# All block products by seven smaller ones, on seeded PSUM quarters, with adds on GpSimd and by DMA

## The chip, the cores and the metric

The kernel runs on one core of one Trainium2 chip. TensorE multiplies (its weight loads have a row of their own, PEld), VectorE (DVE) and ScalarE (ACT) do element-wise work and read and write PSUM, GpSimd (POOL) works on SBUF alone, and SyncE (SP) issues most DMAs; GpSimd and ScalarE issue the others. The metric is the device time in microseconds (us).

## The reference, cut to what matters

Hash attention makes x, of 4 batches x 768 tokens x 512 channels, and an MLP mixer follows, all in fp32:

```python
xt = x.transpose(0, 2, 1)
h = np.maximum(xt @ w_tok1, 0.0) @ w_tok2
u = x + h.transpose(0, 2, 1)
h2 = np.maximum(u @ w_ch1, 0.0) @ w_ch2      # w_ch1 [512, 1536], w_ch2 [1536, 512]
return (u + h2).astype(np.float32)
```

The change is all in the last two products, which the code calls the first and the second channel product.

## The kernel before, in words

The program has three stages: attention, token mixing and channels. Channels keeps u transposed in SBUF as XT (channels on partitions) and goes over its 3072 tokens in three stages s = 0, 1, 2 of 1024 tokens, two halves of 512 (TT).

**Block products.** A product of two matrices is cut in 2 x 2 blocks and made from seven block products, p1 to p7, instead of eight. Left operands are weights or sums of weight blocks (WC1 and SW1 for the first product, WC2 and SW2 for the second), right operands are token blocks or their sums (XT and T[0] to T[3], made by `inputs`). The partial sums come together by adds and by accumulation in PSUM. This can be done again inside a block product: then its left operand is seven smaller pieces, its right one has quarters b00 to b11 and four sums of them, and matmuls have 256 columns instead of 512.

**Stage s = 0, first product.** `hidden(0, t)`, t = 0 to 5, makes one row block of the hidden layer from seven block products of 2 instructions of 512 columns each (L806 to L822), in two pairs of PSUM banks (`blocks(2)`), and writes R[0] to R[3] with rectifiers. Between its parts it runs `jobs` from `prepare` (L1030): two lists of jobs to a t, one in the middle (L818) and one after. A job of `parts` (L1046) makes four sums of a weight's quarters on VectorE in a place, the one buffer `seen` or a free range of another tile, and SyncE stores them and the raw quarters in DRAM. Second-product parts are six (and p1 as a whole copy), first-product parts are the four names in SMALLER.

**Stages 1 and 2, first product.** `hidden_pair(s, t, between)`, t = 0 to 2, makes two row blocks at once: p1, p5 and p7 whole, in 4 instructions of 512 columns each (`whole`, L945), and p2, p6, p3, p4 by seven smaller ones each (class Smaller, L885), whose left pieces `fetch_hidden_left` brings from DRAM on SyncE's queue, five deep.

**Second product.** `outputs(s)` runs seven block products in the order p1, p5, p7, p6, p3, p2, p4. p1 is whole (`whole_product`, L1137, 12 instructions of 512 columns); in s = 0 it uses WC2 where it lies. The others are `product` (L1151): seven parts of 3 instructions of 256 columns in two pairs of banks, copies by ScalarE, adds and right sums by VectorE, and `fetch_left` of the product after the next. Results go to DRAM by accumulating DMAs from GpSimd's queue (`store`).

**Looks.** `look` brings a part of q or k in by a DMA from GpSimd's queue, and ScalarE squares and sums it (L1296, L1297); 32 of them are spread over hidden pairs and products. At the end they decide whether a careful version must run.

**Order.** Each engine runs its instructions in the order in which the code issues them; the waits between engines are put in by the framework, from what each instruction reads and writes. `accumulate` (L776) issues all matmuls of the channel stage, L779 in the profile.

Of the kernel before, what the change touches and what calls it, by code (L numbers as in the profile page):

```python
# [48 lines left out]
def kernel(  # L49
# [13 lines left out]
    nc = tc.nc  # L63
# [687 lines left out]
    def channels(pool, psum, SW1, second, TA, judge):  # L751

        KC, HC, QC = NCB // 2, NHT // 2, NHT // 4
        TB = pool.tile([P, 2, KC, TT], F32, name="TB", tag="TB", bufs=1)
        T = [TA[:, 0], TB[:, 0], TA[:, 1], TB[:, 1]]

        R = [pool.tile([P, 2, HC, TT // 2], F32, name=f"R{i}", tag=f"R{i}", bufs=1) for i in range(4)]
        q1 = pool.tile([P, KC, TT], F32, name="q1", tag="q1", bufs=1)
        last = B * S // (2 * TT) - 1

# [3 lines left out]

        ring = [0, 1, 2, 3]

# [3 lines left out]
        def blocks(n):  # L770

            now = ring[:n]
            ring[:] = ring[n:] + now
            return [bank_pair(i) for i in now]

        def accumulate(ps, left, right, ks, start=True, stop=True):  # L776
            ks = list(ks)
            for k in ks:
                nc.tensor.matmul(  # L779
                    ps, left(k), right(k), start=start and k == ks[0], stop=stop and k == ks[-1],  # L780
                    skip_group_check=True,
                )

        def copy(ps, c):
            nc.scalar.copy(c, ps)  # L785
            return c
# [3 lines left out]

        unfinished = []

        def end_rows():

            if unfinished:
                unfinished.pop()()

        def hidden(s, t):
# [6 lines left out]
            ps = [b[:, i] for b in blocks(2) for i in range(2)]  # L805
# [5 lines left out]
            p1 = copy(ps[0], c[0])  # L811
            p5 = copy(ps[2], c[1])
            accumulate(ps[0], lambda k: SW1[:, 0, k, low], lambda k: T[1][:, k], ks, False)
            p7 = copy(ps[3], c[2])
            end_rows()
            nc.vector.tensor_tensor(r[0], split(ps[1]), split(p1), op=ALU.add)
            nc.vector.tensor_scalar(r[0], r[0], 0.0, None, op0=ALU.max)
            for job in jobs.pop(0) if jobs else []:  # L818
                job()
# [3 lines left out]
            u = copy(ps[0], c[3])  # L823
            for k, a in [(3, p7), (1, ps[2]), (2, ps[3])]:
                nc.vector.tensor_tensor(r[k], split(a), split(u), op=ALU.add)
            nc.vector.tensor_scalar(r[1], r[1], 0.0, None, op0=ALU.max)

            def end():
                for k in (3, 2):
                    nc.scalar.activation(r[k], r[k], ACT.Relu)  # L830

            unfinished.append(end)
            nc.vector.tensor_tensor(r[1], r[1], r[0], op=ALU.subtract)

        def right_sums(name, s):


            sl = [slice(TT * (2 * s + i), TT * (2 * s + i) + TT) for i in range(2)]
            src = {"p2": XT[:, KC:, sl[0]], "p3": XT[:, KC:, sl[1]], "p6": T[1], "p4": T[3]}[name]
            z = split4(XT[:, SMALLER.index(name), : 2 * TT])  # L840
            half = [slice(0, TT // 2), slice(TT // 2, TT)]
            b = [src[:, k, n] for k in range(2) for n in half]

            def job():
                nc.vector.tensor_tensor(z[:, 0], b[1], b[0], op=ALU.subtract)
                nc.vector.tensor_tensor(z[:, 1], b[3], b[1], op=ALU.subtract)
                nc.vector.tensor_tensor(z[:, 2], b[3], z[:, 0], op=ALU.subtract)
                nc.vector.tensor_tensor(z[:, 3], b[2], z[:, 2], op=ALU.subtract)

            return job, [*b, *(z[:, i] for i in range(4))]  # L850

        def split4(a):
            return a.rearrange("p (n t) -> p n t", n=4)

        def fetch_hidden_left(h):

            if h < 4 * GP * last:
                t = h // 4 % GP
                nc.sync.dma_start(
                    out=hidden_left_at(h).rearrange("p (i c) -> p i c", i=7),  # L860
                    in_=hidden_passed[SMALLER[h % 4]][:, :7, P * t : P * t + P],
                )

        def hidden_left_at(h):

            h, n = h % 5, 7 * P
            if h < 3:
                return WC1[:, KC:].rearrange("p k c -> p (k c)")[:, n * h : n * h + n]
            return SW1[:, 2 * (h - 3)].rearrange("p k c -> p (k c)")[:, :n]
# [5 lines left out]
        def first_weight(name):  # L875

            return {
                "p2": WC1[:, KC:, : DCH // 2], "p3": SW1[:, 2], "p4": WC1[:, KC:, DCH // 2 :], "p6": SW1[:, 0],
            }[name]
# [5 lines left out]
        class Smaller:  # L885


            def __init__(self, h, name, s):
                self.h, self.w = h, hidden_left_at(h).rearrange("p (i c) -> p i c", i=7)
                self.b = right_sums(name, s)[1]  # L890

            def one(self, pair, e):

                self.ps, self.e = pair, split4(e)
                self.mm(pair[:, 0, : TT // 2], 4, 0)
                nc.scalar.copy(self.e[:, 0], pair[:, 0, : TT // 2])

            def three(self, pair, start=False):

                self.mm(pair[:, 0, : TT // 2], 5, 2, start)  # L900
                self.mm(pair[:, 0, TT // 2 :], 3, 3, start)
                self.mm(pair[:, 1, : TT // 2], 6, 7, start)

            def rest(self):

                self.mm(self.ps[:, 1, : TT // 2], 0, 4)
                self.mm(self.ps[:, 1, TT // 2 :], 1, 5)
                self.mm(self.ps[:, 0, : TT // 2], 2, 6, False)
                fetch_hidden_left(self.h + 5)

            def mm(self, ps, left, right, start=True):
                accumulate(ps, lambda k: self.w[:, left], lambda k: self.b[right], [0], start)

            def finish(self):

                u = extra_flat()[:, TT // 2 * (self.h % 2) : TT // 2 * (self.h % 2) + TT // 2]
                nc.scalar.copy(u, self.ps[:, 0, : TT // 2])
                p57 = self.ps[:, 1].rearrange("p (n t) -> p n t", n=2)
                nc.vector.tensor_tensor(
                    self.e[:, 1:3], p57, u[:, None, :].to_broadcast([P, 2, TT // 2]), op=ALU.add,  # L920
                )
                nc.vector.tensor_tensor(self.e[:, 3], p57[:, 0], self.e[:, 2], op=ALU.add)

        def hidden_pair(s, t, between):


            sl = [slice(TT * (2 * s + i), TT * (2 * s + i) + TT) for i in range(2)]
            ks = range(KC)
            r = [a[:, :, t::GP].rearrange("p n i c -> p i n c") for a in R]
            x, z, e, y = ring  # L930
            ring[:] = [y, e, x, z]

            p1, e2 = [output_at(i).rearrange("p i n -> p (i n)") for i in (0, 2)]
            p5, e6, u = copies(), copies(), copies()
            e3, e4 = p1, e2
            h = 4 * GP * (s - 1) + 4 * t
            p2, p6, p3, p4 = [Smaller(h + i, name, s) for i, name in enumerate(SMALLER)]

            def rows(a):
                return a.rearrange("p (i n c) -> p i n c", i=2, n=2)  # L940

            def banks(a):
                return a.rearrange("p i (n c) -> p i n c", n=2)

            def whole(pair, left, right, which=(0, 1)):  # L945
                for i in which:
                    at = P * (t + GP * i)
                    accumulate(pair[:, i], lambda k: left(k)[:, at : at + P], right, ks)

            def copy(to, pair):  # L950
                nc.scalar.copy(to.rearrange("p (i n) -> p i n", i=2), pair)

            def plus(to, a, b):
                nc.vector.tensor_tensor(to, a, b, op=ALU.add)

            def relu(i):
                nc.scalar.activation(r[i], r[i], ACT.Relu)

            X = bank_pair(x)
            whole(X, lambda k: WC1[:, k], lambda k: XT[:, k, sl[0]])  # L960
            Z, E = bank_pair(z), bank_pair(e)
            copy(p1, X)
            p2.one(E, e2)
            p2.three(Z, True)
            Y = bank_pair(y)
            whole(Y, lambda k: WC1[:, k, DCH // 2 :], lambda k: T[0][:, k], [0])
            n = TT * 3 // 2
            plus(p1[:, :n], Z.rearrange("p i n -> p (i n)")[:, :n], p1[:, :n])
            end_rows()
            p2.rest()  # L970
            whole(Y, lambda k: WC1[:, k, DCH // 2 :], lambda k: T[0][:, k], [1])
            p2.finish()
            copy(p5, Y)
            look()
            plus(r[0], rows(p1), rows(e2))
            for job in between:
                job()
            E = bank_pair(z)
            p6.one(E, e6)
            p6.three(X)  # L980
            copy(u, X)
            V = bank_pair(e)
            whole(V, lambda k: SW1[:, 1, k], lambda k: T[2][:, k])
            p6.rest()
            look()
# [488 lines left out]
```

## Time and profile before

| | |
|---|---|
| time, median of 3 runs | 797.19 us (797.18 to 799.81) |
| profiled execution: its time, its span | 795.77 us, 794.0 us |
| channel stage on TensorE (chain of waits) | 388.17 to 788.79 us |
| TensorE busy | 786.4 us, 99% of the span |
| VectorE, ScalarE, GpSimd busy | 659.7, 441.4, 53.5 us |
| DMA moved | 138.67 MB, mean 175 GB/s |
| ScalarE copy out of PSUM, 256 / 512 / 1024 columns | 0.37 / 0.59 / 1.01 us |
| VectorE add, 256 / 512 / 768 / 1024 columns | 0.42 / 0.69 / 0.95 / 1.22 us |
| GpSimd add, 512 columns (L820, 6 of them) | 1.26 to 2.57 us, median 1.38 |

A row of the profile names the line, the engine, the operation, the tiles that it writes and reads, the shape and the count, then busy time and the mean of one, then the idle time of the engine just before and what ended it. A matmul's length includes its way through the array, so matmuls overlap.

### The profile page before, as it was taken

The page shows a single profiled execution, that of the slowest core. Times are in us where ns is not written, and L with a number is a line of the kernel's source. Part 1 is how long each engine was busy: PE and PEld are TensorE (multiplying, and loading weights), DVE is VectorE, ACT ScalarE, POOL GpSimd, SP SyncE. Part 2 cuts the span into 40 slices and gives each one's busy share as a digit, 9 for nine tenths or more (in the row PEclk, how much of TensorE's full clock was granted, in tenths as well). Part 3 has the DMA queues.
Part 4 walks back from the last instruction along what each step waited for, and adds up shares of the span by engine and source line. Part 5 has one row for each costly group of instructions (what it writes and reads, how often), then busy time and mean ns, then how long its engine had stood idle before and what let it go on. Part 6 is the DMA issues. An engine that isn't in the chain of part 4 may idle for free.

```text
span 794.0 us, 12166 instructions
## 1 busy us (share of the span) xinstructions
PE 786.4 (99%) x4661; PEld 464.9 (59%) x4661; DVE 659.7 (83%) x885; ACT 441.4 (56%) x706; POOL 53.5 (7%) x77
## 2 busy tenths in 40 slices
PE   8999999999999999999999999999999999999997
PEld 4444444444444444455544458876667886666886
DVE  5989898988987677999688788988769897778986
ACT  6688888888888886333323221327773335775111
POOL 1000000000000000011121010111110012000001
PEclk9999999999999999999999999999999999999999
DMA  4435353538352425796726994699754578730456
GB/s 163 163 123 163 123 163 123 163 122 246 143 178 87 154 47 166 215 281 173 175 60 228 334 356 145 185 294 283 218 148 139 217 204 195 218 109 1 148 176 159
DMA packets 90974, 138.67 MB, mean 175 GB/s; under 512 B 29656, under 2 KB 63392, under 8 KB 88608
## 3 DMA queue, kind: packets, MB, share of 16 engines
q1 hardware_dynamic: 82752, 112.86, 42.9%
q0 software_dynamic: 7728, 24.64, 14.0%
q8 instruction: 38, 0.62, 0.3%
q10 hardware_dynamic: 432, 0.34, 0.2%
q14 instruction: 24, 0.20, 0.1%
HBM read 97.21 MB, written 33.16 MB: 164 GB/s over the span
## 4 chain that ended last, share of the span: by engine, by line
PE 99%; DMA 1%; SPq 0%; DVE 0%; issue 0%
PE b L779 50%; PE sc L353 20%; PE acc L406 16%; PE t L652 5%; PE t L692 5%; PE sums L430 2%; PE hp L301 1%; DMA qk<-in_qk 1%; PE hw L325 0%; SPq L271 0%; DVE second L1202 0%; PE b L1319 0%; SPq L1469 0%
## 5 line engine op out<-in xcount | busy, mean ns | idle before, releaser
L360 ACT ACTIVATE e<-sc 128x768 f32<-128x768 f32 x192 | 154.1, 811 | 11.6 <-PE sc L353 11.2
L353 PE MATMUL sc<-qk 64*128 64x384 f32 x768 | 152.6, 483 | 0.0
L779 PE MATMUL b<-R,second 128*128 128x256 f32 (+1 forms) x612 | 150.9, 404 | 0.0
L779 PEld LDWEIGHTS b<-R,second 128*128 128x128 f32 x612 | 116.3, 190 | 31.6 <-issue 17.2
L785 ACT COPY c<-b 128x512 f32<-128x512 f32 (+1 forms) x78 | 37.4, 488 | 169.2 <-PE b L779 159.6
L406 PE MATMUL acc<-e,vn 128*32 128x384 f32 x1536 | 127.0, 486 | 0.0
L391 DVE TENSOR_TENSOR esd<-esd,e 128x768 f32<-128x768 f32 x96 | 92.0, 958 | 10.4 <-ACT e L360 0.5
L406 PEld LDWEIGHTS acc<-e,vn 128*32 128x32 f32 x1536 | 49.9, 110 | 73.9 <-issue 73.3
L353 PEld LDWEIGHTS sc<-qk 64*128 64x128 f32 x768 | 68.2, 187 | 40.8 <-issue 35.6
L779 PE MATMUL b<-XT,WC 128*128 128x256 f32 (+1 forms) x264 | 82.5, 456 | 0.0
L779 PEld LDWEIGHTS b<-XT,WC 128*128 128x128 f32 x264 | 50.2, 190 | 29.6 <-issue 25.1
L353 PE MATMUL sc<-bits 64*128 64x384 bf16 x384 | 62.5, 323 | 0.0
L387 DVE SCALAR_TENSOR_TENSOR esd<-e 128x768 f32<-128x768 f32 x32 | 30.6, 955 | 24.5 <-ACT e L360 24.5
L652 PE MATMUL t<-x,W 128*128 128x512 f32 x96 | 41.8, 593 | 0.0
L353 PEld LDWEIGHTS <-bits 64*128 64x128 bf16 x384 | 18.7, 94 | 33.0 <-issue 9.0
L712 POOL DMA_DIRECT2D XT<-second x8 | 9.9, 1232 | 386.0 <-DVE second L711 361.6
L451 ACT COPY rec<-rec 32x384 f32<-32x384 f32 x64 | 32.6, 510 | 5.0 <-DVE rec L445 4.2
L412 ACT ACTIVATE num<-acc,vsum 128x384 f32<-128x384 f32 x32 | 18.6, 581 | 29.8 <-PE acc L406 29.4
L779 PE MATMUL b<-XT,SW 128*128 128x256 f32 (+1 forms) x120 | 34.6, 422 | 0.0
L779 PE MATMUL b<-TA,WC 128*128 128x512 f32 x72 | 33.8, 592 | 0.0
L779 PE MATMUL b<-TA,SW 128*128 128x512 f32 x72 | 32.9, 592 | 0.0
L394 DVE TENSOR_TENSOR esd<-esd,e 128x768 f32<-128x768 f32 x32 | 30.5, 954 | 1.9
(217 smaller groups left out, 1129.3 us busy)
## 6 DMA issues: line engine op xcount, KB each, us to landing
second<-left SPq DMA_DIRECT2D x18, 1344.0 KB
raw<-in_moe_w_ch SPq DMA_DIRECT2D x16, 768.0 KB
qk<-in_qk SPq DMA_DIRECT2D x15, 768.0 KB
seen<-in_qk POOLq DMA_DIRECT2D x21, 384.0 KB, 3.8
WC<-hidden_left SPq DMA_DIRECT2D x15, 448.0 KB
vn<-in_v SPq DMA_DIRECT2D x16, 384.0 KB
vt<-in_vT SPq DMA_DIRECT2D x16, 384.0 KB
x<-bounced SPq DMA_DIRECT2D x4, 1536.0 KB
```

The costliest lines, as they stand in the source:

```text
L353: nc.tensor.matmul(sc[:, i, :HALF], t[rows, 1, P * c : P * c + P], t[rows, 0, qs], start=start, stop=not start,)
L360: nc.scalar.activation(e, sc[:, :, :HALF], ACT.Exp, scale=SCALE)
L387: nc.vector.scalar_tensor_tensor(self.d, es[0], NR * EPS, es[1], op0=ALU.add, op1=ALU.add,)
L391: nc.vector.tensor_tensor(self.d, self.d, e, op=ALU.add)
L394: nc.vector.tensor_tensor(self.d, self.d, self.es[-1], op=ALU.add)
L406: nc.tensor.matmul(acc[D * i + d : D * i + d + 32], vn[:, i, c, d : d + 32], e[:, i], start=(c == 0), stop=(c == NR - 1),)
L412: nc.scalar.activation(nums[self.n][:, self.half], acc, ACT.Identity, scale=-1.0, bias=vsum,)
L451: nc.scalar.copy(rec[other : other + 32, h], rec[at : at + 32, h])
L652: nc.tensor.matmul(ps, W1[:, r, P * j : P * j + P], x[:, r], start=(r == 0), stop=(r == NR - 1),)
L692: nc.tensor.matmul(ps[at], left, right, start=start, stop=True, skip_group_check=True,)
L779: nc.tensor.matmul(ps, left(k), right(k), start=start and k == ks[0], stop=stop and k == ks[-1], skip_group_check=True,)
L785: nc.scalar.copy(c, ps)
```

## The change

It does five things.

- **All block products of the first channel product** in stages 1 and 2, and all of the second one in every stage, are made by seven smaller ones. `hidden` of stage 0 stays. Classes Hidden and Second, on a common Product, take the place of `Smaller`, `whole`, `whole_product` and `product`.
- **PSUM:** every product has a (bank 0) and c (bank 1) of one of three pairs, 256 columns each, and b, a quarter of the fourth pair, the forks. ScalarE copies a into b, and b then accumulates from this seed.
- **The order on TensorE** is that of `go(y)`: products of y are interleaved with the last two of x, the product before.
- **Adds:** the halves 2 and 3 of a hidden product are added by GpSimd (`Hidden.end`), quarters 0 and 1 by VectorE straight from PSUM (`head`); more of the output's sums are left to accumulating DMAs (`ends`, `sums`).
- **Preparation:** parts of p1 for the second product and of p1, p5, p7 for the first are added to the jobs in stage 0, up to two in a list; `fetch_left(0)` is now needed and is issued at t = 5, `fetch_left(1)` at t = 4. Looks leave the hidden pairs and are put into gaps of the second product.

```diff
+    def places(self):
+        pair = flow.pair()
+        self.a, self.c, self.b = pair[:, 0, :N], pair[:, 1, :N], flow.seeded()
+        self.copies = copies()
...
+def gap(y, n=1):
+    if flow.gaps:
+        run(flow.gaps[:n])
+        del flow.gaps[:n]
+    elif flow.looks and y.patient:
+        flow.looks -= 1
+        look()
+
+def go(y, work=[], early=[]):
+    x, flow.before = flow.before, y
+    y.places()
+    y.mm(y.a, 4, 0)
+    copy(y.b, y.a)
+    y.mm(y.c, 1, 5)
+    y.first_done()
+    if x:
+        x.mm(x.a, 3, 3, False)
+        x.one()
+    run(early)
+    gap(y, 2 if y.patient else 1)
+    y.mm(y.a, 2, 6, False)
+    y.take(y.u, 2)
+    run(work)
+    y.mm(y.b, 5, 2, False)
+    y.second_done()
+    y.zero()
+    gap(y)
+    if x:
+        x.mm(x.c, 6, 7, False)
+        x.two()
+        x.end()
+    y.mm(y.a, 0, 4, False)
+    y.take(y.u5, 3)
+    y.three()
+    y.spent()
+    gap(y)
...
+    def seeded(self):
+        i = self.quarter = (self.quarter + 1) % 4
+        return self.forks[:, i // 2, N * (i % 2) : N * (i % 2) + N]
...
 sums = weight_sums(WC2, SW2, slice(0, HC), slice(HC, NHT), low, high)
 return [
-    [], sums, [whole("p1"), second_parts("p7")], *([second_parts(name)] for name in ("p6", "p3", "p5", "p2", "p4")),
-    *([hidden_parts(name)] for name in SMALLER),
+    [], sums, [second_parts("p1"), second_parts("p7")], [second_parts("p6")], [second_parts("p3")],
+    [second_parts("p5"), hidden_parts("p1")], [second_parts("p4"), hidden_parts("p2")],
+    [second_parts("p2", True), hidden_parts("p6")], [hidden_parts("p5", True), hidden_parts("p3")],
+    [hidden_parts("p7", True), hidden_parts("p4")],
 ]
...
+plan = dict(
+    p1=([], [e]), p2=([e], [r0]), p6=([e], [u]), p5=([u], [v]), p3=([v], [r1]),
+    p7=([v, u], [r3, w]), p4=([w], [r2]),
+)
...
 for t in range(HC):
...
-    if t == 4 if judge else t == 0:
-        if not judge:
-            fetch_left(0)
+    if t == HC - 2:
         fetch_left(1)
+    if t == HC - 1:
+        fetch_left(0)
+        hidden(0, t, opening(0))
+        break
```

(The diff's indentation is cut by two levels here.) In `go`, `y.take` is ScalarE's copy of a, `y.three` and `x.two` are VectorE's reads of c, `x.one` and `y.zero` take a and b out, `y.first_done` and `y.second_done` make right sums of the second product, and `work` holds sums that later products need: in the first hidden pair of a stage one `right_sums` of four adds for each of p1, p2, p6, p5, in the last p4 the `difference` and the first two sums (`begin`) of the outputs. `True` in a list of jobs means the other place instead of `seen`.

## The prediction

> **What bounds the kernel now.** I read the page first, its chain of waits second, then the stages that the diff touches.
>
> ```profile
> PE 786.4 (99%) x4661; PEld 464.9 (59%) x4661; DVE 659.7 (83%) x885; ACT 441.4 (56%) x706; POOL 53.5 (7%) x77
> ```
> ```profile
> 310.41 20.80 PE t L652 x48
> ...
> 388.17 364.23 PE b L779 x1308
> 752.40 0.11 PE b L1319
> 752.51 36.28 PE b L779 x168
> 788.79 0.02 issue
> ```
>
> The columns of the chain are start, length, what. TensorE never stops from 388.17 to 788.79: the channel stage is 1476 passes in 400.5 us. Each fp32 matmul instruction is two passes: 192 instructions of 512 columns and 546 of 256 give 384 and 1092 passes. If cost follows columns, one 256-column pass costs 400.5 / (2 x 384 + 1092) = 0.215 us; the 512-column passes of L652 cost 20.80/48 = 0.433, twice that. So columns are what is paid for, and a wait of TensorE is paid in full.
>
> Next, how a wait on PSUM works here. In the timeline of one block of the first channel product (start, length, engine, line, count, idle before and releaser):
>
> ```profile
> 395.08 1.07 ACT L785 COPY c<-b 128x512 f32<-128x512 f32 x2 [2.79 <-PE b L779]
> 396.20 0.19 PEld L779 LDWEIGHTS b<-XT,SW 128*128 128x128 f32 x1 [0.28 <-ACT c L785]
> 396.85 0.69 DVE L816 TENSOR_TENSOR R<-b,c 128x512 f32<-128x512 f32 x1 [5.19 <-ACT c L785]
> ```
>
> A weight load at 396.20 belongs to a product into ps[2] (L821). ScalarE's copy of ps[2] is the first of the two at 395.08; the second, of ps[3], ends at 396.15. The load started 0.05 after that second one, though ps[3] is another bank. L816 reads ps[1], ready by 391.6, but starts at 396.85, as the later product into ps[0] ends (388.17 + 10 instructions x 0.86 = 396.8). I read: **the program orders accesses by PSUM tile, not by bank**, and a tile here is a pair of banks.
>
> The price of one hand-over, in a second channel product:
>
> ```profile
> 473.25 0.37 ACT L785 COPY c<-b 128x256 f32<-128x256 f32 x1 [1.63 <-PE b L779]
> 474.08 1.27 PEld L779 LDWEIGHTS b<-second 128*128 128x128 f32 x6
> 474.30 1.46 PE L779 MATMUL b<-second 128*128 128x256 f32 x6
> ```
>
> The passes before 474.30 are six of the third part, so the second part streamed out at 474.30 - 1.29 = 473.01, and the copy started 0.24 later. It takes 0.37. TensorE's restart is 0.05 (above) plus 0.22 from weight load to matmul.
>
> Last, the preparation of the smaller products' left operands inside stage 0 (VectorE, SyncE, then the windows; there the columns after the engines are clock, DMA share, GB/s):
>
> ```profile
> 413.40 0.55 DVE L1056 TENSOR_TENSOR seen<-second 128x384 f32<-128x384 f32 x1
> ...
> 415.05 0.56 DVE L1059 TENSOR_TENSOR seen<-second,seen 128x384 f32<-128x384 f32 x1
> ...
> 425.53 0.56 DVE L1056 TENSOR_TENSOR seen<-second 128x384 f32<-128x384 f32 x1 [2.31 <-DMA left<-seen]
> ```
> ```profile
> 415.64 0.34 SPq L1067 DMA_DIRECT2D left<-seen  x1
> ...
> 422.18 0.34 SPq L1067 DMA_DIRECT2D left<-seen  x1
> ```
> ```profile
> 436.00:460.00 24.00, 24.00 (x57) 10.63 (x56) 17.54 (x34) 6.58 (x12) 3.19 (x3) 1.00 1.01 346
> 460.00:474.00 14.00, 14.00 (x42) 7.74 (x41) 12.15 (x18) 2.65 (x4) 1.09 (x2) 1.00 0.90 335
> ```
>
> One part costs VectorE 2.2 us and its one buffer `seen` is free again 3.35 us after the store's issue (422.18 to 425.53). The DMA engines are already full from 436 to 474.
>
> **The Trainium skill.** "PSUM — Partial Sum Buffer", section "PSUM bank collisions raise a hardware error": engines must be kept apart per bank and quadrant, and different banks run clean. The hardware would allow the overlap that the change wants; the trace shows this program not using it. "DMA: Bandwidth & Descriptors", "Specifications": a ceiling of 435 GB/s; the trace agrees, 346 over that stage. "ScalarE: Activation LUTs", "Step-by-step": ScalarE writes PSUM faster than SBUF; no row of before shows it, so 0.37 us is taken for the seed and 0.30 kept as lower bound, 0.45 as upper. "TensorE: Matmul & The Clock Gate", "Part 1": after an idle window of 3.4 us the clock halves, for about as long; no run here has such a window; an estimate from it is 1.7 us for one long stop.
>
> **The change part by part.**
>
> *Columns removed.* In hidden_pair p1, p5, p7 were 4 instructions of 512, 16 pass units; seven block products are 14. Two fewer x 3 products x 6 pairs = 36. In outputs p1 was 48 units, now 42: 6 x 3 = 18. 54 x 0.215 = **-11.6 us**, on the path.
>
> *Seeds.* `go` issues product 4, ScalarE's copy from a into a quarter of the forks, then product 1 into c. a and c are two banks of one pair, so product 1 waits for that copy: 0.24 + 0.37 + 0.05 + 0.22 = 0.88 us with nothing else in TensorE's queue allowed past it. 49 matmuls of a pair make 7 products, so 42 products in stages 1 and 2 and 21 in the outputs: 63 x 0.88 = **+55.4**. Bounds of the copy: 63 x 0.81 to 0.96, 51 to 60.
>
> *ScalarE work ahead of a seed.* `go` ends with the u5 copy and a gap; the next seed queues behind what fills it. A look is 0.85 + 0.94 + 0.19 = 1.97 us. In outputs ScalarE is free 0.24 + 0.37 + 1.97 = 2.58 after the last product's stream, the seed's source after 1.29 + 0.24 = 1.53: 1.05 late. 32 looks at three gaps a product put about 10 there: **+10.5** (5 to 18). In hidden pairs a rectifier (0.58 a half) is there three times a pair: 0.24 + 0.37 + 0.59 = 1.20 against 0.43 + 0.24 = 0.67, 0.53 x 18 = **+9.5** (3 to 14). The looks' other time lies beside 21 products of 9.0 us.
>
> *VectorE.* The copy out of a quarter stands behind `work`, and the next seed, in the same forks tile, behind it. Four right sums (4 x 0.42) per product in four products of t = 0 make it about 0.45 late each; the `begin` (2 x 0.95) with the difference ahead of outputs 1.1. 2 x (1.6 + 1.1) = **+5.5** (2 to 14). Elsewhere VectorE has room: some 8.4 of 9.9 us at most in outputs.
>
> *GpSimd and DMA adds.* 7 adds a pair at 1.38 us are 10 us in 27, hidden; if they stretch (one took 2.57 beside VectorE) the rectifier after them waits. Accumulating stores grow from 4 to 8 a stage on GpSimd's queue, 1.22 us each: hidden, since the looks behind them are fetched three ahead. At the end q3's store waits for q5's on the same rows (8.4 us to land), about 2 us before the last one: nothing.
>
> *Preparation, on the path.* Stage 0 now prepares 14 parts instead of 10, two in most slots, and all must pass SyncE's one queue before `fetch_left(0)`, which the first output product needs; before, that product used WC2 where it lay. VectorE: p1 at 413.4, then 2.2 + 3.35 a part where `seen` is reused: p7 419.0, p6 424.5, p3 430.0, p5 435.5, hidden p1 441.0, p4 446.5, hidden p2 452.0. The R adds of t = 3 (2.9) end at 457.0, so t = 5 stalls about 5 us; p2 457.0 and p6 459.1 follow, p5 462.5, p3 466.3, R adds, p7 473.5, p4 477.5 to 479.6, then the opening sums 3.8. Bytes: from hidden p2's store on (454.5) six hidden parts of 1536 KB, p2 of 1344 and two fetches of 1344: 13.5 MB at 346 to 392 GB/s is 34 to 39 us, so operand 0 lands near 490. Stage 0 ended at 388.2 + 84 x 0.86 = 460.2: **+30** (15 to 40), and 1.7 for the cold clock.
>
> *Tail.* In `go_last` the last product into c waits for a VectorE read of a (0.24 + 0.42 + 0.27), and fewer adds follow: **+0.5**.
>
> Sum: -11.6 + 55.4 + 10.5 + 9.5 + 5.5 + 30 + 1.7 + 0.5 = **+101.5**. The profiled execution took 795.8 us, 794.0 of it span; 795.8 + 101.5 = 897.3. The median is 797.2, 1.4 above: I say **898**. This case's own range, from the bounds: 845 to 940.
>
> **Rivals.**
> 1. *Waits by bank.* The two seed waits fall away, product 1 and x's product cover the copy (0.86 against 0.66), and looks and VectorE cost 3. Preparation still holds: 797.2 - 11.6 + 31.7 + 3 = 820. For it: the banks are kept apart with care. Against: 396.20 and 396.85 above. Range 808 to 830.
> 2. *TensorE stays the bound (not slower).* The whole price is columns: 797.2 - 11.6 = 786. The place is the start of outputs(0): it decides if operand 0 lands within 11.6 us of 460.2, by 472, and no seed is waited for. Against: 22.8 MB now pass from 415.6 (seven parts of 1344 KB, seven of 1536, two fetches); by 472 that needs 415 GB/s throughout with no pause for `seen`.
> 3. *GpSimd joins the chain.* 42 adds at 2.57 us instead of 1.38 are 50 us more, 948 if none of it stays hidden. For: the stretched row, and rectifiers on ScalarE that wait for an add stand ahead of seeds. Against: one row of six, and 18 us a pair would still fit in 27.
>
> **How the numbers follow.** Forecast 0.76, rival 1 0.14, rival 2 0.05, rival 3 0.05. Eight in ten: leave out rival 2, half of rival 1 and the upper end: 818 to 930. Faster by over 0.5% (about what this kernel's measurement tells from no change) 0.04, within 0.01, slower 0.95.
>
> **What would show it.** TensorE's share falls from 99% to about 87%. Rows of a ScalarE copy b<-b 128x256, 63 of them, release about 0.6 us of idle weight loads each; in a window of hidden pairs a product takes 3.9 us instead of 3.0. After 460 TensorE idles some 25 us, ended by the DMA of `left` or by VectorE's opening sums. The forecast is wrong if the second matmul of a product follows the first with no gap, or if outputs(0) starts by 472.

## The result and the profile after

The kernel before took 798.07 us (median of 6 runs, 797.18 to 799.81), the changed one **942.99 us** (median of 6, 937.9 to 948.21): ratio 1.1814, 95% interval 1.177 to 1.1859. The forecast was 898, and 930 the upper end of the range that was given eight chances in ten. The direction was right, but 45 us are missing from the sum.

The page of the changed kernel, its busy times and two of the rows in 40 slices (busy tenths of TensorE, then its granted clock in tenths):

```profile
PE 814.7 (87%) x4823; PEld 499.1 (53%) x4823; DVE 648.3 (69%) x964; ACT 460.9 (49%) x830; POOL 122.1 (13%) x130
...
PE   9999999999999999999708882788888966888995
...
PEclk9999999999999999999859996899999987999998
```

TensorE was busy for 99% of the span before. Now it has 87% of 940.4 us, and the clock falls in the slices where it stopped. The share alone, forecast as "about 87%", does not say where. The windows do (start and end, length, then busy us of PE, PEld, DVE, ACT and POOL with their counts, clock, DMA share, GB/s):

```profile
471.00:494.00 23.00, 0.97 (x2) 0.83 (x3) 13.62 (x21) 0.59 (x1) 1.09 (x2) 0.56 0.98 380
494.00:568.00 74.00, 64.35 (x276) 53.72 (x275) 47.97 (x64) 43.90 (x89) 13.17 (x19) 0.95 0.77 231
568.00:592.50 24.50, 1.77 (x9) 1.21 (x7) 2.28 (x6) 4.27 (x8) 6.00 (x7) 0.60 0.98 271
...
754.00:859.00 105.00, 78.88 (x310) 59.88 (x311) 47.22 (x109) 33.31 (x86) 28.35 (x23) 0.92 0.41 103
```

There are two long stops, one ahead of outputs(0) (471 to 493) and one at the start of the hidden pairs of s = 1 (568 to 592.5). The hidden pairs of s = 2 (754 to 859) take 105 us for 79 us of matmul.

The waits of the changed kernel name the causes (engine and line, what it waited for, us in total, times, longest):

```profile
PEld b L777 <- ACT b L783: 108.8, 63, 23.2
...
POOL out L1287 <- issue: 47.5, 9, 10.2
...
PE b L777 <- DMA second<-left: 23.5, 1, 23.5
...
ACT looked L1379 <- DMA looked<-in_qk: 16.7, 1, 16.7
...
ACT R L793 <- POOL R L1039: 12.8, 12, 5.1
```

The first is the seed wait, 63 times, as forecast. Its four longest are stops of another origin (23.17, 7.16, 4.59 and 4.24 us); without them it is 69.6 us over 59, 1.18 each. The third is operand 0 of outputs(0). The second was not in the forecast: GpSimd's queue, where an accumulating store (L1287) waited nine times for nothing that the profile names.

One ordinary seed in a hidden pair, in the timeline of the changed kernel: ScalarE's copy b<-b, and the weight load and matmul that waited for it.

```profile
603.41 0.36 ACT L783 COPY b<-b 128x256 f32<-128x256 f32 x1
603.82 1.16 PEld L777 LDWEIGHTS b<-XT,WC 128*128 128x128 f32 x6 [0.85 <-ACT b L783]
603.82 1.35 PE L777 MATMUL b<-XT,WC 128*128 128x256 f32 x5 [0.45 <-ACT b L783]
```

The copy takes 0.36 us, 0.37 was assumed; the weight load stood still for 0.85, where 0.88 was put.

The stop at 568, from the same timeline, GpSimd's queue first and then who waits:

```profile
556.95 1.26 POOL L1287 DMA_DIRECT2D out<-second  x1 [0.20 <-issue]
566.02 1.22 POOL L1287 DMA_DIRECT2D out<-second  x1 [7.81 <-issue]
...
575.45 1.20 POOL L1287 DMA_DIRECT2D out<-second  x1 [8.21 <-issue]
576.16 1.11 POOL L1390 DMA_DIRECT2D looked<-in_qk  x1
583.22 1.19 POOL L1287 DMA_DIRECT2D out<-second  x1 [5.95 <-issue]
583.86 0.84 ACT L1379 ACTIVATE looked<-looked 128x768 f32<-128x768 f32 x1 [16.70 <-DMA looked<-in_qk]
...
592.53 0.50 PEld L777 LDWEIGHTS b<-WC 128*128 128x128 f32 x2 [23.17 <-ACT b L783]
```

Read it downwards. Accumulating stores stand in the queue together, and each is issued 8 to 9 us after the one before. The look behind the third comes at 576.16, right after it. ScalarE, which runs its instructions in the order of issue, wants that look and waits 16.70 us for its data. A second look holds it again at 590. The seed copy stands behind both on ScalarE, and TensorE behind the seed.

The profile calls the time between the stores "issue" and names nobody, but the trace has a time that fits: the landing of the store ahead, the moment when its DMA reports its end. For the store of 556.95:

```profile
DMA to landing us min/median/max: 8.7/8.7/8.7
```

It landed at 565.69, and the second store was issued at 566.02. The next two landed at 575.11 and 582.91, and the stores behind them were issued at 575.45 and 583.22. In the kernel before and in every run whose stores accumulate, none of them was issued before the accumulating store ahead of it on GpSimd's queue had landed, and those that stood waiting came 0.3 to 0.4 us after that.

At the end of the kernel the chain of waits runs through such landings (start, length, what):

```profile
885.36 1.22 DMA out<-second
886.58 9.12 issue
...
895.72 1.21 POOL out L1287
896.94 9.73 issue
...
906.68 8.17 DMA second<-XT
...
920.80 9.74 PE b L777 x36
```

The last residual (`add_residual`, itself accumulating) goes into q7, which the store of 895.72 reads, so it has to wait for that store whatever kind it is: run 4, below, shows this wait too. Here the store took 10.6 us to land, the one in run 4, which does not accumulate, 6.7. VectorE's sums, a seed and the last products follow.

### The profile page after: what moved, and what is told of

It is laid out like the page before. It is cut to its first block, busy times and chain, and to the rows that moved or that the text cites. A ratio compares the mean times of both kernels' runs of the same rounds, so it can differ in the third digit from the quotient of the medians.

```text
span 940.4 us, 12941 instructions
## 1 busy us (share of the span) xinstructions
PE 814.7 (87%) x4823; PEld 499.1 (53%) x4823; DVE 648.3 (69%) x964; ACT 460.9 (49%) x830; POOL 122.1 (13%) x130
## 5 line engine op out<-in xcount | busy, mean ns | idle before, releaser
L777 PE MATMUL b<-R,second 128*128 128x256 f32 x594 | 140.7, 389 | 24.8 <-DMA second<-left 23.5
L783 ACT COPY c<-b 128x256 f32<-128x256 f32 (+1 forms) x146 | 58.3, 406 | 179.1 <-PE b L777 144.4
L391 DVE TENSOR_TENSOR esd<-esd,e 128x768 f32<-128x768 f32 x96 | 92.0, 958 | 10.4 <-ACT e L360 0.5
L777 PE MATMUL b<-XT,SW 128*128 128x256 f32 (+1 forms) x208 | 65.9, 429 | 13.9 <-ACT b L783 13.9
L777 PE MATMUL b<-XT,WC 128*128 128x256 f32 (+1 forms) x164 | 56.9, 460 | 8.0 <-ACT b L783 8.0
L777 PEld LDWEIGHTS b<-XT,SW 128*128 128x128 f32 x208 | 40.0, 199 | 31.9 <-ACT b L783 19.5
L787 DVE TENSOR_TENSOR R<-b,second 128x256 f32<-128x256 f32 x48 | 20.3, 423 | 44.5 <-PE b L777 44.5
L787 DVE TENSOR_TENSOR R<-R 128x768 f32<-128x768 f32 x45 | 44.7, 1002 | 8.7 <-PE b L777 8.1
L777 PE MATMUL b<-WC 128*128 128x256 f32 x56 | 19.1, 426 | 30.2 <-ACT b L783 26.6
L793 ACT ACTIVATE R<-R 128x512 f32<-128x512 f32 x48 | 29.9, 632 | 27.9 <-DVE R L787 15.1
```

The source lines that it names most:

```text
L391: nc.vector.tensor_tensor(self.d, self.d, e, op=ALU.add)
L777: nc.tensor.matmul(ps, left(k), right(k), start=start and k == ks[0], stop=k == ks[-1], skip_group_check=True,)
L783: nc.scalar.copy(to, ps)
L787: nc.vector.tensor_tensor(to, a, b, op=op)
L793: return lambda: nc.scalar.activation(a, a, ACT.Relu)
```

## The experiments

Each is an edit of the changed kernel (943.0 us), run 9 of that of run 7. Times are medians; the ratio is to the kernel before, run on the same chip.

### 1. Every PSUM bank its own tile

```diff
-return psum.tile([P, 2, TT], F32, name=f"b{i}", tag=f"b{i}", bufs=1)
+return [psum.tile([P, TT], F32, name=f"b{i}{j}", tag=f"b{i}{j}", bufs=1) for j in range(2)]
```

> Edit: each of the eight PSUM banks is a tile of its own, the order of all instructions stays. Theory (waits are by PSUM tile): product 1 no longer waits for the seed copy, so 63 waits of about 0.9 us, and what looks and rectifiers ahead of the copies add, leave TensorE: 943 - 55 = 888 us, between 870 and 900, and the group of ScalarE's copy b<-b releases almost no idle weight loads. Rival (the seed itself is late whatever the tiles are, because ScalarE comes late to it): over 930 us.

**888.8 us**, 1.1149 (1.11 to 1.1198). The theory holds: 54 us went by cutting the tiles apart alone, with every instruction where it was. From the waits and the timeline of this kernel:

```profile
PEld b L777 <- ACT b L783: 12.6, 17, 4.2
```
```profile
601.37 0.41 PEld L777 LDWEIGHTS b<-WC,SW 128*128 128x128 f32 x2
...
601.58 0.59 PE L777 MATMUL b<-WC,SW 128*128 128x256 f32 x2
...
601.78 0.36 ACT L783 COPY b<-b 128x256 f32<-128x256 f32 x1
```

Product 1 is loaded at 601.37 and runs from 601.58, before the seed copy has begun, and no idle time stands at either. In this run ScalarE reads one bank and writes another while TensorE writes a third, so the wait came from the program.

### 2. The seed copy issued after product 1

```diff
-            copy(y.b, y.a)
             y.mm(y.c, 1, 5)
+            copy(y.b, y.a)
```

> Edit: in go and go_last ScalarE's seed copy is issued after product 1 instead of ahead of it; tiles stay pairs. Theory (waits are by tile): product 1 no longer waits, the copy waits for product 1 as well, and the next writer of the pair, product 2, waits for the copy. x's product lies between: 1.29 us in outputs covers the hand-over of 0.88, 0.43 in hidden pairs leaves 0.45. 21 x 0.88 + 42 x 0.43 = 36 us less: 907, between 890 and 915. Rival (waits by bank): nothing waited for the copy before, so the time stays within 3 us of 943.

**905.2 us**, 1.1347 (1.1308 to 1.1387), 38 us off where 36 were worked out. With waits by bank this edit would have given nothing, so it is a second and independent sign that waits go by tile. It also fits the price of one hand-over, since the 36 came from 0.88 and from what x's product covers.

### 3. The looks on ScalarE's queue

```diff
-                nc.gpsimd.dma_start(out=t, in_=qk[pairs[n][0], pairs[n][1], :, i])
+                nc.scalar.dma_start(out=t, in_=qk[pairs[n][0], pairs[n][1], :, i])
```

> Edit: the DMAs of the looks are issued from ScalarE's queue instead of GpSimd's. Theory (the looks are held on GpSimd's queue behind the accumulating stores of the outputs): the stop of TensorE at 568 to 592 in the profile, 24 us, falls away, ScalarE pays up to 32 short issues: 921 us, between 912 and 928. Rival (the looks come late because the DMA engines are full): the stop stays, 938 to 948. Second rival: the stop only moves to what else stands behind the stores on GpSimd's queue, 930 to 940.

**945.9 us**, 1.1861 (1.1818 to 1.1904): no gain. The time lies in the range of the first rival, but the timeline doesn't give its reason:

```profile
567.05 1.22 POOL L1287 DMA_DIRECT2D out<-second  x1 [8.53 <-issue]
...
569.21 0.37 ACT L783 COPY c<-b 128x256 f32<-128x256 f32 x1 [5.21 <-DMA SW<-hidden_left]
...
576.94 1.21 POOL L1287 DMA_DIRECT2D out<-second  x1 [8.67 <-issue]
...
606.00 0.63 ACT L793 ACTIVATE R<-R 128x512 f32<-128x512 f32 x1 [5.75 <-POOL R L1039]
...
606.94 0.50 PEld L777 LDWEIGHTS b<-WC,SW 128*128 128x128 f32 x2 [4.62 <-ACT c L783]
```

Three things are to be seen. With no look between them, the stores still come 9.7 to 10.7 us apart, so the looks do not make the gaps. The stop at 568 has gone, but what else stands behind the stores is late in its place: GpSimd's adds, then the rectifier of 606.00, then TensorE. And ScalarE, which now issues the looks (0.33 to 0.36 us each), became late for seeds: a weight load behind a look mostly waits 2.1 to 2.4 us in outputs(0), where it mostly waited 1.64, and at 569.21 ScalarE stood 5.21 us until a DMA that SyncE had issued was done. That wait is an instruction of the program: it stands ahead of the look's issue at 568.83 and is for the semaphore that the look's own DMA uses next. From first matmul to first matmul, outputs(0) grew from 76.1 to 89.6 us, while the hidden pairs of s = 1 fell from 108.6 to 98.0.

### 4. Stores apart, without accumulation

```diff
                     nc.gpsimd.dma_start(
-                        out=out[KC * i : KC * i + KC, :, sl[n]].rearrange("m p t -> p m t"), in_=q,
-                        accum_op=ALU.add,
+                        out=scratch, in_=q,
                     )
```

> Edit: the eight accumulating stores a stage go to memory of their own and add nothing, so none waits for another; the outputs then lack the second channel product in the rows that these stores make. Bytes written are the same, and the reads of the accumulation are gone. Theory (each accumulating store to the same rows waits some 8 us for the one before, and looks, the last residual and GpSimd's adds queue behind it): the stops at the start of hidden pairs s = 1 (24 us) and s = 2 (16) and the one of outputs(2) (6) go: 943 - 45 = 898 us, between 890 and 910. Rival (bytes and full DMA engines): 930 or more, with the stops still there, shorter by the reads alone.

**904.0 us**, 1.1338 (1.1294 to 1.1382), 39 us off for 45 worked out; the output lacks the sums of these stores. From first matmul to first matmul the hidden pairs of s = 1 take 96.9 us (108.6 in the changed kernel), those of s = 2 84.3 (102.3). What remains at s = 1 had been hidden beneath:

```profile
578.97 2.90 PE L777 MATMUL b<-R,second 128*128 128x256 f32 x6 [6.54 <-DMA second<-left]
```

Here the rest of the last output product's left operand is late, which is fetched behind 3.6 MB of hidden pieces on SyncE's queue.

### 5. Stores to the same rows, overwriting

Edit 4 changed two things, so this one changes one: the stores keep their rows, their order and their waits and lose only `accum_op`.

```diff
                         out=out[KC * i : KC * i + KC, :, sl[n]].rearrange("m p t -> p m t"), in_=q,
-                        accum_op=ALU.add,
```

> Edit: the eight stores a stage go to the same rows of the output as in the changed kernel, in the same order and with the same waits, but overwrite instead of accumulating (the output is then only the last of each). It tells apart why stores hold GpSimd's queue. Theory A (an accumulating store holds the queue until the one before it has landed, whatever rows it goes to): GpSimd issues the stores within about 1.3 us of each other, the stops go as with stores apart, 904 us, between 898 and 912. Theory B (the wait is for the same rows of the output, as the prediction said): two or three of the stores still wait some 8 us, 915 to 940.

**900.7 us**, 1.1316 (1.1271 to 1.1361). This is what theory A said. In the timeline the same stores as at 556.95 to 583.22 above:

```profile
554.04 2.15 POOL L1287 DMA_DIRECT2D out<-second  x3 [0.16 <-issue]
...
561.55 0.71 POOL L1287 DMA_DIRECT2D out<-second  x1 [1.95 <-DMA out<-second]
```

Three go out within 2.15 us. The fourth goes to rows of an earlier one and waits 1.95 us, named as a DMA. The second and the third were issued 6.1 and 7.3 us before the one ahead had landed. So it is accumulating that makes a store wait for the landing, whatever the rows; the wait for the same rows is small. The stores' reads of the output went away as well, so a share for bytes can't be split off, but the landing time changed only from a median of 8.1 to 6.7 us.

### 6. Ten parts in stage 0

```diff
-                [], sums, [second_parts("p1"), second_parts("p7")], [second_parts("p6")], ...
-                [second_parts("p5"), hidden_parts("p1")], [second_parts("p4"), hidden_parts("p2")],
+                [], sums, [second_parts("p7")], [second_parts("p6")], ...
+                [second_parts("p5")], [second_parts("p4"), hidden_parts("p2")],
...
+    second["passed"]["p1"] = second["passed"]["p7"]
```

> Edit: stage 0 prepares the ten parts that it prepared before the change, without p1 of the second product and p1, p5, p7 of the first; those four products then use the pieces of other names, so the result is not the reference's, but every instruction and fetch of the later stages is there. Theory (preparation is on the path at the end of stage 0): outputs(0) starts near 472 instead of 493, 943 - 20 = 923 us, between 915 and 930. Rival (the opening sums or the fetch of operand 0 are late anyway): less than 8 us, over 935.

**922.7 us**, 1.1585 (1.1547 to 1.1622), 20 us off, as expected.

```profile
475.29 2.04 PE L777 MATMUL b<-R,second 128*128 128x256 f32 x4 [14.66 <-DMA second<-left]
```

outputs(0) starts at 475.3 instead of 493.0. A stop of 14.7 us is left with the old number of parts. The kernel before, which used operand 0 where WC2 lay, started outputs(0) at 460.1, so the rest goes with the way through DRAM. Whether an earlier fetch of it would help was not tried: `fetch_left(0)` is issued last in stage 0.

### 7. Edits 1, 4 and 6 together

> Edit: three at once, every bank a tile of its own, stores apart without accumulation, ten parts in stage 0 (what these leave out is said where each was run alone). If the causes add up: 889 - 39 - 20 = 830 us, between 820 and 842, which is some 32 above the kernel before. If waits by tile covered others (a shorter stage leaves less time for stores, fetches and GpSimd), less is gained: 842 to 870. If they overlap the other way (one stop had two causes, both needed to go), below 820.

**834.9 us**, 1.0469 (1.0439 to 1.0499). The three causes are nearly independent: singly they gave 54.2, 39.0 and 20.3 us, in sum 113.5, together 108.1. What is left above the kernel before is 38 us. Most of it is in two stops:

```profile
474.31 2.21 PEld L777 LDWEIGHTS b<-R,second 128*128 128x128 f32 x6 [14.49 <-DMA second<-left]
...
553.54 2.90 PE L777 MATMUL b<-R,second 128*128 128x256 f32 x6 [14.63 <-DMA second<-left]
```

The second is the stop of run 4 behind SyncE's queue, now longer since less lies above it. Together they are 29 us; the other 9 were not taken apart.

### 8. GpSimd's adds on VectorE

```diff
-                    nc.gpsimd.tensor_tensor(
+                    nc.vector.tensor_tensor(
                         to(slice(2, 4)), split(self.copies[:, 2 * N :]), a(slice(2, 4)), op=ALU.add,
```

> Edit: the adds of halves 2 and 3 of a hidden product go to VectorE instead of GpSimd; all else stays. Rival 3 of the prediction (GpSimd's adds are in the chain: rectifiers wait for them, seeds for the rectifiers) expects 20 us or more off: under 925. My theory (the adds are late only where they stand behind stores at the start of a stage; 12 waits of ScalarE for them, 12.8 us in all, partly beside other stops): 5 to 12 us off, 931 to 938. VectorE has 42 adds of 0.69 us more, 29 us of its idle time; if that delays seeds, 943 or more.

**942.1 us**, 1.1817 (1.1787 to 1.1847): no difference from the changed kernel. In its waits the rectifier's row has become the first of these, and the second is new:

```profile
ACT R L793 <- DVE R L1039: 3.0, 8, 0.6
PEld b L777 <- DVE c L787: 7.3, 16, 0.8
```

12.8 us of waiting became 3.0, and the time stayed. In part the rectifiers were late beside stops with other causes (the weight load at 768.26 still waits 7.03 us for a seed). In part VectorE, with 42 adds more, now holds TensorE itself: 7.3 us in 16 short waits that the changed kernel does not have. So a gain of about that size may be hidden here. The third reading, that VectorE delays TensorE, came nearest; the 20 us or more of rival 3 are not there.

### 9. Hidden pieces fetched later, on top of run 7

```diff
-                if s == 0:
-                    work["p2"] += [lambda h=h: fetch_hidden_left(h) for h in range(8)]
+                work["p4"] += [*([lambda h=h: fetch_hidden_left(h) for h in range(8)] if s == 0 else []), ...
```

> Edit: as with the three edits together, and the eight fetches of hidden left pieces in outputs(0) are issued in the last output product (p4) instead of the one before it (p2), so they stand behind the rest of p4's own left operand on SyncE's queue. Theory (the 15 us stop at 538 to 553 in the profile of the three edits is p4's own operand behind 3.6 MB of hidden pieces): 835 - 13 = 822 us, between 817 and 827. Rival (full DMA engines, whatever the order): the stop moves to the first hidden product, over 830.

**828.6 us**, 1.0364 (1.0334 to 1.0395): 6 us off (8 by the ratios, as it ran on another chip than run 7), about half of the 13.

```profile
547.20 1.19 PE L777 MATMUL b<-XT,WC 128*128 128x256 f32 x2 [6.99 <-DMA WC<-hidden_left]
```

The stop of 15 us is now one of 7, at the first hidden product, which waits for its own pieces. So both readings hold in part: order on the queue was worth half, the bytes due at that moment the rest.

### 10. Everything computed, fewer accumulating stores

Banks apart, the later fetch, all fourteen parts, and adds by VectorE in place of four of the eight stores:

```diff
-            sums = [add(q7, q7, q6), add(q5, q5, q6)]
-            sums += [store(q5, 0, 1), *([store(q7, 1, 0), store(q7, 1, 1)] if more else [store(q6, 1, 1)])]
+            sums = [add(q5, q5, q6), add(q6, q6, q7), add(q7, q7, q5), store(q7, 1, 1)]
...
-                p3=[store(q3, 0, 1)],
+                p3=[add(q3, q3, q5), store(q3, 0, 1)],
...
-                nc.gpsimd.dma_start(out=q7, in_=XT[:, KC:, sl[0]], accum_op=ALU.add)
+                nc.gpsimd.tensor_tensor(q6, q6, XT[:, KC:, sl[0]], op=ALU.add)
```

> Edit: a version that computes everything, with all fourteen parts: every bank a tile of its own, the later fetch of hidden pieces, and in each output stage four accumulating stores (three or fewer at the last) instead of eight (five); p1 + p2 and the sums of q5, q6, q7 and q3 are added by VectorE, the last residual by GpSimd. Theory: the start of outputs(0) stays near 491 (+31 against the kernel before), the stops by stores go but for some 5 us, VectorE's extra adds cost 5: 889 - 39 - 6 + 5 = 849 us, between 840 and 862, still slower than before. Rival (VectorE, with about 8 us more a stage, becomes the bound in outputs): over 865.

**866.3 us**, 1.0855 (1.082 to 1.089): 77 us better than the changed kernel, 17 worse than expected, and just inside the range of the rival (over 865). From its waits:

```profile
PEld b L777 <- DVE c L787: 17.6, 5, 6.2
```

Five times TensorE waits for VectorE, in p2 and p4, where the new adds and the in-place sums stand: 17.6 us, as much as the whole miss, though no run took this wait out alone. What the DMAs had taken off VectorE goes back on it, and there it is late. No run here points to a version below the kernel before: even run 9, which leaves work out, is 30 us above it.

## Why the prediction was wrong

**The step that failed** is the first half of *GpSimd and DMA adds*: "Accumulating stores grow from 4 to 8 a stage on GpSimd's queue, 1.22 us each: hidden, since the looks behind them are fetched three ahead." The 1.22 is the length of the issue. What counts is the distance to the next one: an accumulating store waits for the landing of the one ahead, and in the changed kernel's rows it comes 6.1 to 11.4 us after it. Four or five stores that come together hold the queue for 26 to 33 us (556.95 to 583.22 and to 589.45), and three looks ahead last one product, about 10. The term was put at nothing; run 4 measured 39 us and run 5 42. With 42 in its place the sum is 898 + 42 = 940, against 943. That it closes so well is in part luck, since other terms were off both ways, as below. The same part spoke of a wait "on the same rows"; run 5 shows that rows hardly matter.

The sign was there before. The 8.4 us to landing was used for the tail alone, and not for the stores inside the stages. And the timeline of the kernel before has two accumulating DMAs of token mixing on the same queue, the first of which took 8.6 us to land:

```profile
376.77 1.21 POOL L712 DMA_DIRECT2D XT<-second  x1 [7.12 <-DVE second L711]
385.68 1.22 POOL L712 DMA_DIRECT2D XT<-second  x1 [7.70 <-issue]
```

**Columns, -11.6.** No run measured it alone. Where the waits are mostly gone it is not to be seen: the hidden pairs and outputs of s = 2 take 138.0 us in run 7 (68.9 and 69.2), 132.2 before (67.2 and 65.0).

**Seeds, looks, rectifiers, +75.4 in sum.** Right as a wait: the forecast is 75.4/63 = 1.20 us a seed, the waits give 1.18. In time, run 1 returned 54 of it. That adds, stores and VectorE hold the rest of what is freed is likely, and not shown.

**Preparation, +30.** Right in kind: operand 0 "near 490" came at 493.0, and TensorE's row names the DMA of `left`. Measured it is +32.9, of which four parts are 17.7 (493.0 to 475.3); the rest goes with the way through DRAM. The Trainium skill's ceiling of 435 GB/s ("DMA: Bandwidth & Descriptors", "Specifications") was approached: the stop moved 380 GB/s at a DMA share of 0.98.

**Cold clock, 1.7.** The windows show a clock of 0.56 and 0.60 in the two stops. The first six passes after the first one take 2.90 us and the next six 2.20, where six take 1.46 in the undisturbed product of before: 2.2 us for this stop. The estimate from the Trainium skill ("TensorE: Matmul & The Clock Gate", "Part 1") was about right for one stop, but there were two long ones.

**VectorE, +5.5, and the tail, +0.5.** VectorE stayed small until runs 8 and 10 loaded it. The tail was put too small: behind two stores that land slowly, the residual cost a stop of 4.59 us. In run 4's last stage the longest wait for a seed is 1.51.

**Rivals.** Waits by bank: refuted by runs 1 and 2. TensorE stays the bound: refuted by the result. GpSimd joins the chain: its 948 lies nearest to 943, yet its mechanism, slower adds, does not carry it (run 8). GpSimd joined by its queue, not by its arithmetic. A number that fits does not prove the story that gave it.

## What to carry to other kernels

Price a DMA on a queue by its distance to the next one, which the landing can set, and not by the length of its issue, and list all that stands behind it on that queue and on the engine that waits for it; accumulating stores bunched at the end of a stage are the case to look for first. A copy that only touches one bank can still hold back a matmul to the next: look at how the tiles are cut before trusting that two banks overlap, and cut them apart, which here was worth 54 us. When work is taken off one engine by a DMA, ask where in time the DMAs bunch, and when it is put back, whether the engine still has the time in that very product.

## What was not expected of the hardware

- Two accumulating DMA stores of 512 KB in a row on GpSimd's queue are issued 6.1 to 11.4 us apart in the changed kernel and in run 3, to different rows too, and the second comes 0.3 us after the first has landed. Plain ones follow after 0.72 us (run 5), and a plain load right after an accumulating store is issued 0.7 us after it (575.45 and 576.16). What makes the queue wait for the landing is not shown: the profile puts it down to "issue", and the trace has no wait of the program that ends there (566.02 to 583.22).
- ScalarE's copy within PSUM takes 0.36 us for 256 columns, hardly less than one from PSUM to SBUF (0.37). The 0.30 that the prediction kept as a lower bound did not come.
- Issuing the looks' DMAs from ScalarE cost outputs(0) 13.5 us at about three looks a product, more than their rows of 0.33 to 0.36 us add up to; the wait of 5.21 us, which the program makes, is part of it.
